# Transposing a block's gradient row into two PSUM banks, and issuing two zero fills earlier

## The chip, the cores and the metric

The kernel runs on one NeuronCore of a Trainium2 chip. The metric is the device time of one execution in microseconds. A core has a matrix engine (PE), a vector engine (DVE), a scalar engine (ACT), a general engine (POOL) and a queue engine (SP). Each takes its instructions in order. Transfers between device memory and the on-chip memory (SBUF) are carried by 16 DMA engines, which serve a queue that POOL fills and a queue that SP fills. Results of PE land in PSUM, which has eight banks of 2 KB per partition.

## The reference

One decode step of a conditioned transformer block with a single token, forward and backward. The token's vector has 1024 elements. A vector `c` gives six modulation vectors; attention of 32 heads over the last 4096 of 65536 cached positions (4 key and value heads) follows, then a gated feed-forward part with 3584 hidden units.

```python
def _B_ref(x, w_gate, w_up, w_down):
    g = jnp.einsum('bsd,df->bsf', x, w_gate)
    u = jnp.einsum('bsd,df->bsf', x, w_up)
    h = _sigmoid(g) * u
    return jnp.einsum('bsf,fd->bsd', h, w_down)
mod = (_silu(c) @ w_mod).reshape(c.shape[0], 6, 1, -1)
...
h = _layernorm(x, axis=-1) * (1 + ca) + sa
x = x + ga * _A_ref(h, A_k_cache, A_v_cache, A_wq, A_wo)
h = _layernorm(x, axis=-1) * (1 + cb) + sb
x = x + gb * _B_ref(h, B_w_gate, B_w_up, B_w_down)
...
_out, _vjp = jax.vjp(_f, A_x, A_k_cache, A_v_cache, A_wq, A_wo, B_w_gate, B_w_up, B_w_down, c, w_mod)
_grads = _vjp(grad_out)
```

The outputs are the block's output and the gradients of ten inputs. The gradients of the two caches have the shape of the whole caches, 2 x 4 x 65536 x 128 elements in bf16, and are zero outside the last 4096 positions. Writing these zeros is most of the kernel's traffic.

## The kernel before

The code is written out by hand in program order, and each engine runs its share in that order. One large SBUF array, `arena`, holds all big tiles at fixed offsets, so a tile that is to be written again waits for the transfer that reads it.

**Zero fills.** `zero(n, after)` takes the next `n` regions from one list, `zleft`, and issues each as a POOL transfer (L209) of 1 MB from an SBUF tile of zeros to device memory. At six places of the list stands a narrow region: a counter reset, a transfer of 2.5 KB (L194) and one of 960 KB (L197). With `after` given, the fill waits for that instruction. The tables at the top (`Z_FFN`, `Z_ROWS`, `Z_HAND` and others) say how many fills are issued at each place. A fill earlier in the program therefore means one fewer at the place where the list ends.

**Feed-forward turns.** The hidden units are cut into seven blocks of 512. For each block `q`, `load_ug` (L965, POOL) brings its columns of w_up and w_gate in four transfers of 512 KB, into one of two buffers, and `load_wd` (L954, SP) brings its rows of w_down in two. `front(q)` (L1053, PE) multiplies the gate and up columns with the vector `h2`. `turn(q)` then makes the gates, transposes three of the eight row groups of the loaded weights (`turned`, L1076), sums w_down times the output gradient on DVE (`wd_ttr`, L253, into the tile `dhh`), and calls `dug_part(q)`.

**The gradient row.** `dug_part` computes eight columns `dug` (four for up, four for gate), turns each into a row that stands on all 128 partitions by a PE transpose of a broadcast column (L1111), and copies the result from PSUM to the SBUF tile `dug_b` (which is the tile `scr` in the profile). ACT copies the first 512 elements (L1113) and DVE the second 512 (L245). In the turns, PSUM tiles for such work come from two banks in turn (`new_tp`, with `rot` holding `psum` and `prq`). The transposes of other tiles that fill idle PE time are called side units (`side`, L939 on PE, L940 on ACT).

After the turn, DVE multiplies five of the row groups of the block's weights with `dug_b` and sums them (L253 into `dh2acc`). That frees the block's buffer, and the loads of block `q + 2` are issued. The loop issues fills between them:

```python
            if j == 3:
                if q + 2 < NB:
                    load_ug(q + 2, 0, 4, (0,))
                    zero(Z_FFN[q][0])
                    load_ug(q + 2, 0, 4, (1,))
...
        if q + 2 < NB:
            load_ug(q + 2, 4, 4, (0,))
            zero(Z_FFN[q][1])
            load_ug(q + 2, 4, 4, (1,))
            turn(q + 1, Z_FFN[q][2])
```

In `turn`, the fills of its argument are issued as `zero(fills, wd_ttr(2, 3))`, behind the last w_down sum.

**End stage.** After the seventh block the kernel writes the weight gradients: outer products on DVE (L249) followed by POOL stores, `dwd` (L1138), `dw_rows` (L1130), `dwo` (L1265), then the modulation gradients `sec` (L1260), the gradients of the caches (L1308 for values, L1304 for keys) and of wq. `zero(Z_ROWS[i])` stands behind the i-th of several `dw_rows` calls: `Z_ROWS[0]` behind the second one (about 449 us in the profile) and `Z_ROWS[1]` behind the third (about 459 us).

Of the kernel before, what the change touches and what calls it, by code (L numbers as in the profile page):

```python
# [10 lines left out]
P = 128  # L11
# [11 lines left out]
FB = 512  # L23
# [30 lines left out]
Z_N = spread(33, 128)  # L54
Z_B = [n + (i in (31, 38)) for i, n in enumerate(spread(29, 43))] + [1, 1, 1, 1, 0] + [1, 0, 0, 1, 1, 1, 0, 0] + [1, 0, 1, 0, 1, 0, 0, 0]
Z_FOLD = (1, 1, 2, 3)
Z_FFN = [(1, 0, 1)] + [(1, 1, 1)] * 4 + [(0, 2)]
Z_HAND = (1, 2, 1, 1, 1)
Z_ROWS = (1, 1, 0, 0, 0, 0, 0, 0)
JT = 3  # L60
JV = KD - JT
@with_exitstack
def kernel(
# [26 lines left out]
    nc = tc.nc  # L90
# [17 lines left out]
    def vt(shape, name, dt=FP32):  # L108
        return pool.tile(shape, dt, name=name)
# [13 lines left out]
    ident_bf = vt([P, P], "ident_bf", BF16)  # L123
# [61 lines left out]
    def zero(n, after=None, big=False):  # L185
        for _ in range(n):
            if len(zleft) <= keep[0]:
                return
            region, narrow_ = zleft.pop(0)
            first = None  # L190
            if narrow_:
                nc.gpsimd.inc_swdge_sem([], [], mode="reset_dge_cursor")
                n = nlen - ncount.pop()
                first = nc.gpsimd.dma_start(  # L194
                    out=rest[0:NS, 0:nlen * 128].rearrange("p (t x) -> p t x", t=2)[:, :, n * 64:(n + 1) * 64],
                    in_=zeros[0:NS, 0:64].rearrange("p (t x) -> p t x", t=1).broadcast_to([NS, 2, 64]))
                ins = nc.gpsimd.dma_start(  # L197
                    out=region[8:P, :].bitcast(FP32).rearrange("(t p) x -> p t x", t=2),
                    in_=zeros[0:60, :].rearrange("p (t x) -> p t x", t=1).broadcast_to([60, 2, ZW // 2]))
            elif 119 - len(zleft) in UNEVEN:  # L200
                first = ins = uneven(region)
            elif big and region.shape[0] == 1:
                ins = nc.gpsimd.dma_start(  # L203
                    out=as_rows(region, BIGP).bitcast(FP32),
                    in_=zero_src[:, 0:P * ZW // 4].rearrange("i (p x) -> (i p) x", p=BIGP).bitcast(FP8))
            else:
                if region.shape[0] == 1:
                    region = as_rows(region, P)
                ins = nc.gpsimd.dma_start(out=region.bitcast(FP32), in_=zeros[:, :])  # L209
            if after is not None:  # L210
                dep(first or ins, after)
# [5 lines left out]
    def next_pool():  # L217
        nrot[0] += 1
        return rot[nrot[0] % len(rot)]
# [11 lines left out]
    def new_tp(name="tp"):  # L231
        p, tag = next_pool()
        return p.tile([P, 1024], BF16, name=name, tag=tag)
# [4 lines left out]
    def mulv(out, a, b):  # L238
        return tt(out, a, b, ALU.mult)
# [4 lines left out]
    def cp(out, a):  # L244
        return nc.vector.tensor_copy(out=out, in_=a)  # L245
# [94 lines left out]
    def bcast(col_bf, ncols, out_bf, engs):  # L340
        for k, j0 in enumerate(range(0, ncols, 4)):
            ps = new_ps("bc_ps")
            for jj in range(4):
                nc.tensor.matmul(ps[:, jj * P:(jj + 1) * P],
                                 lhsT=col_bf[:, j0 + jj:j0 + jj + 1].broadcast_to([P, P]), rhs=ident_bf[:, :],
                                 start=(jj == 0), stop=(jj == 3), skip_group_check=True)
            o = out_bf[:, j0 * P:(j0 + 4) * P]
            if engs[k % len(engs)] == "A":
                last = nc.scalar.copy(out=o, in_=ps[:, :])
            else:  # L350
                last = cp(o, ps[:, :])
        return last
# [229 lines left out]
    for tb in range(4):  # L582
# [3 lines left out]
        tp = new_tp("tp_pT")  # L586
# [7 lines left out]
    last = nc.vector.reciprocal(out=rsum, in_=ssum)  # L594
# [318 lines left out]
    v = A3_ps[:, 0:48].rearrange("p (j n) -> p j n", j=KD)  # L913
# [48 lines left out]
    def load_ug(q, j0, n, ks=(0, 1)):  # L962
        for k in ks:
            view = (wu_view, wg_view)[k]
            nc.gpsimd.dma_start(out=ug_tile(q, k, j0, n), in_=ug_part(view, q, j0, n))  # L965
# [72 lines left out]
    dug_b = scr  # L1038
# [66 lines left out]
    def dug_part(q):  # L1105
        dug = dug_all[:, 8 * q:8 * q + 8]
        mulv(dug[:, 0:4], small["dhh"], small["sg"])
        mulv(dug[:, 4:8], small["dhh"], small["hom"])
        tp = new_tp("tp_dug")
        for i in range(8):  # L1110
            nc.tensor.transpose(tp[:, i * P:(i + 1) * P], dug[:, i:i + 1].broadcast_to([P, P]), ident_bf[:, :])  # L1111
        o, v = dug_b.rearrange("p (k f i) -> p k f i", k=2, i=4), tp.rearrange("p (k i f) -> p k f i", k=2, i=4)
        nc.scalar.copy(out=o[:, 0, :, :], in_=v[:, 0, :, :])  # L1113
        return cp(o[:, 1, :, :], v[:, 1, :, :])

    dug_row = [ar(o, 7) for o in (24, 152)]
    def dug_rows(k):
# [9 lines left out]
    def dw_rows(k, j, off, outer):  # L1127
        t = ar(off, 7)
        outer(t, h2[:, j:j + 1], dug_row[k])
        nc.gpsimd.dma_start(out=(dwu_view, dwg_view)[k][:, j, :], in_=t)  # L1130

    def dwd(q, off, outer):
        t = ar(off, 8).rearrange("p (i d) -> p i d", i=4)
        for i in range(4):
            outer(t[:, i, :], hh_all[:, 4 * q + i:4 * q + i + 1], b1k)

        def store():
            nc.gpsimd.dma_start(out=wd_dram(out_8, q), in_=t)  # L1138
        return store
# [7 lines left out]
    def turn(q, fills=0):  # L1147
        gates()
        turned(q, range(JT - 1))
        wd_ttr(0)  # L1150
        hh_ops(q)
        first = wd_ttr(1)
        ffn_mm(q, 0)
        if q + 1 < NB:
            load_wd(q + 1, 0, 2)
        ffn_mm(q, 2)
        turned(q, (JT - 1,))
        side(1)
        zero(fills, wd_ttr(2, 3))
        if q + 1 < NB:  # L1160
            load_wd(q + 1, 2, 2)
        last = dug_part(q)
        turned_mm(q)
        side(1)
        return first, last
# [6 lines left out]
    for q in range(NB):  # L1172
# [8 lines left out]
        for j in range(JT, KD):  # L1181
            w = ug_flat(q, j)
            ttr(w, w, dug_b, dh2acc[:, q * JV + j - JT:q * JV + j - JT + 1])
# [5 lines that stand above are left out]
                elif more:  # L1189
                    zero(Z_FFN[q][1])  # L1190
                    dwd(0, 24, outer_dve)()
# [4 lines left out]
# [5 lines that stand above are left out]
        elif more:  # L1201
# [23 lines left out]
    dw_rows(0, 1, 16, outer_dve)  # L1225
    zero(Z_ROWS[0])
    bcast(dattn_bf, KD, dattn_b, "V")
# [34 lines left out]
    def dwo(u):  # L1262
        for a in range(4):
            outer_dve(wo_t[u][:, a, :], o_perm[:, 8 * a + u:8 * a + u + 1], dattn_b)
        nc.gpsimd.dma_start(out=wo_dram(out_5, u), in_=wo_t[u])  # L1265
# [50 lines left out]
    for b in range(2):  # L1316
        do4 = new_ps("do4")
        for i in range(KD):
            for a in range(4):
# [4 lines left out]
                       in_=do4.rearrange("q (a h r) -> q a h r", a=4, h=4))  # L1324
# [6 lines left out]
    dw_rows(0, 2, 40, outer_dve)  # L1331
    zero(Z_ROWS[1])
    dwo(2)
# [14 lines left out]
    dw_rows(0, 4, 32, outer_dve)  # L1348
    zero(Z_ROWS[2])
    dwo(3)  # L1350
    dw_rows(0, 5, 176, outer_dve)
    dw_rows(0, 6, 160, outer_dve)
    zero(Z_ROWS[3])
    dw_rows(0, 7, 40, outer_dve)
# [10 lines left out]
    dw_rows(1, 0, 64, outer_dve)  # L1365
    zero(Z_ROWS[4])
    dw_rows(1, 1, 72, outer_dve)
# [9 lines left out]
    dw_rows(1, 2, 80, outer_dve)  # L1377
    zero(Z_ROWS[5])
    dw_rows(1, 3, 16, outer_dve)
# [136 lines left out]
```

## Time and profile before

| What | Value |
|---|---|
| median of three runs | 594.79 us (594.39 to 596.32) |
| the profiled execution: its own time | 594.57 us |
| its span, first to last instruction | 592.8 us |
| PE, DVE, ACT, POOL busy | 430.4, 354.9, 248.1, 145.9 us |
| transfers | 246.58 MB, mean 416 GB/s |
| read from and written to device memory | 79.17 MB and 185.60 MB |
| 1 MB zero fills L209 | 42, median 12.6 us from issue to landing |
| transposes of `dug` (L1111) | 56, first at 329.6 us, last at 430.8 us |

The profile is one execution; its times are counted from the start of the span. Transfers are counted per queue and per issuing line, and the time from issue to landing includes the wait behind transfers that were issued before. A line number can be that of a helper: L245 is every DVE copy, L249 every scaled outer product, L253 every multiply-and-sum.

### The profile page before, as it was taken

Reading aid. Unit: us, or ns where it says so; the run is one execution under the profiler, and the core shown is the slowest. Engines: PE = TensorE matmul, PEld = TensorE weight load, DVE = VectorE, ACT = ScalarE, POOL = GpSimd, SP = SyncE. Lnnn points to the kernel's source line nnn. Section 1 sums busy time; section 2 is a strip of 40 time slices with the busy share of each in tenths; the row PEclk is TensorE's granted clock in tenths of the full one; section 3 lists DMA queues with packets and bytes.
Section 4 is the critical chain, followed back from the end, with each engine's and each line's share of the span. In section 5 each row is a group of like instructions: output and inputs, shape, how many; then the busy total and the mean of one; then the engine's idle time right before and its main releaser. Section 6 shows DMA issues by size and latency. Waiting matters only on the chain.

```text
span 592.8 us, 10216 instructions
## 1 busy us (share of the span) xinstructions
PE 430.4 (73%) x4196; PEld 245.4 (41%) x4196; DVE 354.9 (60%) x647; ACT 248.1 (42%) x398; POOL 145.9 (25%) x251
## 2 busy tenths in 40 slices
PE   3997789999999999997977757776655446084510
PEld 2784433333334545543544545555442445013100
DVE  3665679988930102039373866887986869536750
ACT  2579511554540103411224635665671455093410
POOL 3112213122122212122222331323222433213100
PEclk9998689999999999998998757777785658555555
DMA  8999999999999999999999999999999999999997
GB/s 348 421 420 421 422 465 426 425 422 429 426 404 461 417 438 421 410 420 435 427 395 409 418 412 407 397 408 410 423 422 426 424 425 425 422 408 418 414 417 302
DMA packets 32048, 246.58 MB, mean 416 GB/s; under 512 B 4782, under 2 KB 4782, under 8 KB 16689
## 3 DMA queue, kind: packets, MB, share of 16 engines
q0 software_dynamic: 27008, 226.51, 94.8%
q1 hardware_dynamic: 4944, 19.41, 9.2%
q8 instruction: 33, 0.54, 0.4%
q14 instruction: 15, 0.11, 0.0%
q10 hardware_dynamic: 48, 0.01, 0.0%
HBM read 79.17 MB, written 185.60 MB: 447 GB/s over the span
## 4 chain that ended last, share of the span: by engine, by line
PE 35%; DMA 33%; DVE 16%; ACT 6%; issue 6%; POOL 1%; ACTq 0%; POOLq 0%; DVEq 0%
DMA out_dram<-arena 12%; PE b_ps L796 11%; PE n_ps L737 9%; DMA arena<-in_w_mod_dram 6%; DMA arena<-in_B_w_gate_dram 5%; DVE arena L249 4%; PE t_ps L685 4%; DMA out_dram<-out_dram 3%; DVE arena L253 3%; DMA arena<-in_B_w_up_dram 3%; ACT arena L524 2%; DVE scr L253 2%; DVE arena L236 2%; DMA arena<-in_B_w_down_dram 2%; PE tp_k L503 1%
## 5 line engine op out<-in xcount | busy, mean ns | idle before, releaser
L796 PE MATMUL b_ps<-arena 128*128 128x512 bf16 x512 | 118.6, 384 | 1.1 <-ACT arena L940 1.1
L940 ACT COPY arena<-tp_side 128x1024 bf16<-128x1024 bf16 x62 | 60.9, 1017 | 53.0 <-PE tp_side L939 52.2
L236 DVE TENSOR_TENSOR arena<-arena 128x2048 bf16<-128x2048 bf16 x64 | 77.7, 1224 | 8.8 <-PE n_ps L737 5.1
L796 PEld LDWEIGHTS <-arena 128*128 128x128 bf16 x512 | 49.0, 99 | 58.0 <-issue 5.4
L737 PE MATMUL n_ps<-arena 128*128 128x512 bf16 x256 | 67.7, 389 | 3.4 <-DVE arena L236 2.9
L203 POOL DMA_DIRECT2D out_dram<-out_dram x72 | 35.7, 496 | 127.4 <-PE n_ps L737 57.3
L939 PE MATMUL tp_side<-ident_bf,arena 128*128 128x128 bf16 x496 | 50.6, 270 | 9.6 <-DVE arena L236 5.3
L939 PEld LDWEIGHTS <-arena 128*128 128x128 bf16 x496 | 42.0, 124 | 18.4 <-issue 9.1
L1295 PE MATMUL ps_kv<-arena 32*128 32x512 bf16 x64 | 26.6, 581 | 27.6 <-DVE arena L257 11.7
L693 ACT CAST arena<-t_ps 128x512 bf16<-128x512 f32 x56 | 28.9, 598 | 39.9 <-PE t_ps L685 39.9
L1299 ACT ACTIVATE arena<-ps_kv 128x512 bf16<-128x512 f32 x48 | 25.0, 714 | 39.6 <-PE ps_kv L1295 20.5
L253 DVE CUSTOM_DVE_ANT_0 arena<-arena,scr 128x1024 bf16<-128x1024 bf16 x35 | 40.8, 1218 | 0.2
L737 PEld LDWEIGHTS <-arena 128*128 128x128 bf16 x256 | 21.4, 99 | 35.6 <-issue 19.4
L209 POOL DMA_DIRECT2D out_dram<-zeros x42 | 23.2, 554 | 52.4 <-DVE rows_all L236 22.9
L253 DVE CUSTOM_DVE_ANT_0 scr<-arena,b1k 128x1024 bf16<-128x1024 bf16 x28 | 34.2, 1222 | 2.8 <-DMA arena<-in_B_w_down_dram 2.4
L245 DVE CAST arena<-b_ps 128x512 bf16<-128x512 f32 x6 | 4.1, 692 | 50.2 <-PE b_ps L796 50.2
L249 DVE TENSOR_SCALAR arena<-arena,h 128x3584 bf16<-128x3584 bf16 (+1 forms) x24 | 28.3, 1191 | 7.9 <-DMA out_dram<-arena 7.8
L685 PE MATMUL t_ps<-arena 128*32 128x512 bf16 x256 | 24.1, 399 | 2.8 <-ACT arena L760 2.8
L1295 PEld LDWEIGHTS <-arena 32*128 32x128 bf16 x64 | 6.8, 112 | 46.2 <-issue 45.4
L249 DVE TENSOR_SCALAR arena<-arena,cs_col 128x4096 bf16<-128x4096 bf16 (+1 forms) x16 | 16.0, 1015 | 15.2 <-DMA out_dram<-arena 15.2
L524 ACT COPY arena<-tp_wq 128x1024 bf16<-128x1024 bf16 x23 | 21.4, 1066 | 7.3 <-PE tp_wq L522 7.3
L1077 ACT COPY arena<-tp_ug 128x1024 bf16<-128x1024 bf16 x21 | 20.5, 1008 | 6.7 <-PE tp_ug L1076 6.7
(326 smaller groups left out, 660.3 us busy)
## 6 DMA issues: line engine op xcount, KB each, us to landing
out_dram<-zeros POOLq DMA_DIRECT2D x42, 1024.0 KB, 12.6
out_dram<-arena POOLq DMA_DIRECT2D x35, 1024.0 KB, 15.0
out_dram<-arena POOLq DMA_DIRECT2D x16, 896.0 KB, 17.3
arena<-in_A_wq_dram POOLq DMA_DIRECT2D x8, 1024.0 KB, 21.0
arena<-in_A_wo_dram POOLq DMA_DIRECT2D x8, 1024.0 KB, 13.3
arena<-in_w_mod_dram POOLq DMA_DIRECT2D x7, 1024.0 KB, 19.0
arena<-in_B_w_up_dram POOLq DMA_DIRECT2D x14, 512.0 KB, 11.5
arena<-in_B_w_gate_dram POOLq DMA_DIRECT2D x14, 512.0 KB, 14.5
```

Source lines behind the costliest of these rows:

```text
L203: ins = nc.gpsimd.dma_start(out=as_rows(region, BIGP).bitcast(FP32), in_=zero_src[:, 0:P * ZW // 4].rearrange("i (p x) -> (i p) x", p=BIGP ...
L236: return nc.vector.tensor_tensor(out=out, in0=a, in1=b, op=op)
L249: return nc.vector.tensor_scalar(out=out, in0=a, scalar1=s1, scalar2=None, op0=op0)
L253: return nc.vector.tensor_tensor_reduce(out=out, in0=w, in1=b, scale=1.0, scalar=0.0, op0=ALU.mult, op1=ALU.add, accum_out=acc)
L524: nc.scalar.copy(out=blk, in_=tp[:, :])
L685: nc.tensor.matmul(ps[32 * hh:32 * hh + 32, :].rearrange("p (j m) -> p j m", j=4), lhsT=N_sb[:, h * P + a:(h + 1) * P - 3 + a:4], rhs=a4[: ...
L693: nc.scalar.copy(out=o, in_=v)
L737: mm = nc.tensor.matmul(nbank[k][:, :], lhsT=k_nat[:, g, t_ * DH:(t_ + 1) * DH], rhs=vp[:, t_ % 2, 4 * k:4 * k + 4, :].rearrange("p h d -> ...
L796: mm = nc.tensor.matmul(bbank[p][k][:, :], lhsT=a4[:, p, h, :], rhs=wo_t[u][:, a, k * 512:(k + 1) * 512], start=(i == 0 and a == 0), stop= ...
L939: nc.tensor.transpose(tp[:, i * P:(i + 1) * P], blk[:, i * P:(i + 1) * P], ident_bf[:, :])
L940: nc.scalar.copy(out=blk if dst is None else dst, in_=tp[:, :])
L1295: nc.tensor.matmul(ps[:, :], lhsT=rows[r, t8 * P:(t8 + 1) * P], rhs=bd[r, :], start=True, stop=True, tile_position=(32 * tc_, 0))
```

## The change

`dug_part` takes two PSUM tiles in place of one. Four transposes go into the first, and ACT copies it; four go into the second, and DVE copies it. Instructions, shapes and destinations stay the same; the source rows are now in different banks.

Two entries of the fill tables change. Turn 1 and turn 2 issue two fills instead of one behind their w_down sums, and the two fills behind the second and third `dw_rows` are no longer issued. The total stays the same. As all fills come from one list in order, the regions written in between shift by one or two places, two of the narrow ones among them.

```diff
-Z_FFN = [(1, 0, 1)] + [(1, 1, 1)] * 4 + [(0, 2)]
+Z_FFN = [(1, 0, 2), (1, 1, 2)] + [(1, 1, 1)] * 3 + [(0, 2)]
 Z_HAND = (1, 2, 1, 1, 1)
-Z_ROWS = (1, 1, 0, 0, 0, 0, 0, 0)
+Z_ROWS = (0, 0, 0, 0, 0, 0, 0, 0)
...
         mulv(dug[:, 4:8], small["dhh"], small["hom"])
-        tp = new_tp("tp_dug")
-        for i in range(8):
-            nc.tensor.transpose(tp[:, i * P:(i + 1) * P], dug[:, i:i + 1].broadcast_to([P, P]), ident_bf[:, :])
-        o, v = dug_b.rearrange("p (k f i) -> p k f i", k=2, i=4), tp.rearrange("p (k i f) -> p k f i", k=2, i=4)
-        nc.scalar.copy(out=o[:, 0, :, :], in_=v[:, 0, :, :])
-        return cp(o[:, 1, :, :], v[:, 1, :, :])
+        o = dug_b.rearrange("p (k f i) -> p k f i", k=2, i=4)
+        for k in range(2):
+            tp = new_tp("tp_dug")[:, 0:FB]
+            for i in range(4):
+                nc.tensor.transpose(tp[:, i * P:(i + 1) * P], dug[:, 4 * k + i:4 * k + i + 1].broadcast_to([P, P]),
+                                    ident_bf[:, :])
+            v = tp.rearrange("p (i f) -> p f i", i=4)
+            last = nc.scalar.copy(out=o[:, k, :, :], in_=v) if k == 0 else cp(o[:, k, :, :], v)
+        return last
```

The new code is three lines longer, so a line behind it has a number that is 3 higher in the changed kernel (L1265 becomes L1268).

## The prediction

> **What bounds the kernel now.** I read the transfers first, because the table of slices has every engine idle for part of the time and the transfers never.
>
> ```profile
> DMA  8999999999999999999999999999999999999997
> GB/s 348 421 420 421 422 465 426 425 422 429 426 404 461 417 438 421 410 420 435 427 395 409 418 412 407 397 408 410 423 422 426 424 425 425 422 408 418 414 417 302
> ```
>
> Each digit is the busy share of the 16 DMA engines in one fortieth of the span (14.8 us). Only the first and the last slice are under nine tenths. So the span is about bytes over rate: 246.58 MB at the mean of 416 GB/s is 592.7 us of the 592.8. An edit that leaves the bytes alone can only change the rate, or a gap in the stream.
>
> Next the stretches around the change: PE, PEld, DVE, ACT and POOL busy, then granted clock, DMA share and GB/s.
>
> ```profile
> 340.00:360.00 20.00, 11.95 (x164) 9.68 (x164) 11.42 (x26) 8.64 (x10) 6.16 (x9) 0.57 1.15 415
> 360.00:380.00 20.00, 13.10 (x224) 10.68 (x222) 17.79 (x37) 14.20 (x20) 4.64 (x7) 0.80 1.11 397
> 380.00:400.00 20.00, 15.11 (x220) 12.61 (x221) 15.35 (x34) 11.79 (x16) 5.97 (x9) 0.67 1.13 407
> 440.00:460.00 20.00, 10.50 (x107) 5.40 (x107) 15.21 (x47) 5.34 (x5) 5.57 (x9) 0.66 1.07 425
> ```
>
> The feed-forward turns (about 320 to 444) move 397 to 415 GB/s, the start of the end stage 425. Then the chain of waits in the turns, start and length in us:
>
> ```profile
> 357.23 15.78 DMA arena<-in_B_w_gate_dram
> 373.00 0.04 issue
> 373.04 1.10 PE fg L1053 x16
> ...
> 380.56 1.05 PE tp_dug L1111 x8
> 381.61 0.03 ACTq L1113
> 381.63 0.04 issue
> 381.67 0.59 ACT scr L1113
> 382.27 0.02 issue
> 382.29 0.70 DVE scr L245
> ...
> 390.42 14.39 DMA arena<-in_B_w_gate_dram
> ```
>
> A turn starts when its gate weights land, runs to the free buffer, and asks for the weights of two blocks later. Half of this loop is a transfer of 512 KB that takes 14 to 16 us, although 512 KB at 425 GB/s is 1.2 us: it stands in line behind what was issued before it. Its landing is set by the line, not by the moment of its issue. Last, how long the line is (issue to landing, shortest, median, longest):
>
> ```profile
> DMA to landing us min/median/max: 7.1/10.2/15.8
> DMA to landing us min/median/max: 10.7/12.0/14.6
> DMA to landing us min/median/max: 17.0/17.3/17.9
> ```
>
> These are the weight loads L965 from 349 to 412, the zero fills L209 from 440 to 462, and the row stores L1130 from 478 to 512. The line never empties. It is shortest, 7.1 us, for the load issued at 370.19, and full from about 470: there POOL issues one store per 2.44 us, mostly released by an earlier store's landing.
>
> **The change, part by part.**
>
> *Two banks.* Per turn PE makes the same eight transposes (1.05 us together), ACT the same copy (586 ns), DVE the same copy (692 ns). Before, the DVE copy starts when the ACT copy ends (382.29 against 381.67); the built program of the changed kernel makes it wait for PE instead. It can start at about 381.67, and ACT's some 0.5 us earlier. That takes 382.29 - 381.67 = 0.62 us out of each of 7 turns, 4.3 us of chain. Two copies at once from two banks run undisturbed where the trace has them: 597 ns on ACT and 683 on DVE for the ps_kv banks. The second tile takes the other of the two rotating banks, whose last user is the side unit's copy (378.79 to 379.81), done before the transposes at 380.56: no new wait there. If that copy were late, PE and the 24 small matmuls of `turned_mm` behind it would wait up to one such copy, 1.0 us a turn; DVE would still be ahead or even. What is late next? The weights. The freed buffer lets POOL issue L965 0.62 us earlier into a line 7 to 16 us long, so it lands when its place comes up. In turns 1 to 4 I count nothing. From 404.85 on the chain is DVE's to 443, so turns 5 and 6 do bring 2 x 0.62 = 1.2 us of earlier stores; these join a line of 8.3 us at its shortest there (the store of 434.39), so the end gets nothing.
>
> *Two fills moved.* A 1 MB fill takes the line 2.44 us. The second one in turn 1 goes in behind that of 346.68, the second one in turn 2 behind that of 365.89; POOL spends 0.56 us on each, and both stand before loads that POOL cannot issue for 3.7 us more (its idle time <-DVE dh2acc). All fills come from one list, so the 960 KB fill with its small extra transfer moves from 380.6 to 370.9, ahead of a gate load: 0.7 us more of POOL, hidden by the line. The loads behind land 2.44 us later after turn 1 and 4.9 later after turn 2, and the gates wait for them, so the turns end 4.9 - 1.2 = 3.7 us later. SP's w_down loads have their own queue, wait for the same sums, and shift along.
>
> Then the end stage has 4.9 us less to move: POOL no longer issues the fills of 449.62 and 459.20. All bytes ahead of the store of 460.18 are the same in both kernels, so from there on the stream stands at the same absolute time, if it was never empty. Is it? At 449 to 460 the line is 10.7 to 14.6 us; less 4.9 it is at least 5.8. DVE is 100% busy from 460 to 470 and then waits for landings (2.05, 1.30 and 0.26 us up to 478.70), which is where its lateness is absorbed; what is left meets the 17 us line. So the two 4.9 us cancel. The bounds of this term are -0 and +3.7 (nothing given back); I take 0, since its nearest row is the line of 5.8 us that stays.
>
> *The thin place.* From 366 to 376 the stream moves 386 GB/s, against 411 in the nine us before and 406 in the fourteen after (408 weighted): (408 - 386) x 10 / 408 = 0.54 us lost. The extra fills stand just there. Between 0 and 0.54 us I take 0.5.
>
> The end is that of the slowest of the 16 engines: after the POOL queue's last landing at 587.1 the SP queue's last store lands at 591.9, and in the end stage the 16 completions of a store are spread over 4.2 us. If only the leaders ran thin at 366 to 376, the 0.5 us is not theirs to give, and the term is 0. The Trainium skill ("DMA: Bandwidth & Descriptors", Latency and other measured facts) says that engines 7 and 15 are usually slower than the others in traces. By that rule the sum would be 594.6 instead of 594.1; the spread agrees with unequal engines, and no row here names them.
>
> **Sum.** The profiled execution took 594.57 us, its span 592.8 and 1.77 around it; the median of the three runs is 594.79. 594.57 - 0.5 (thin place) + 0 (fills) + 0 (copies) = 594.1. A measurement of this kernel tells about 0.3%, 1.8 us, from no change.
>
> **Rivals.**
>
> *Faster: the turns are thin throughout.* From 320 to 420 the stream moves 407 GB/s on average against 425 after: 100 x 18 / 425 = 4.2 us lost. If that comes from short lines and not from the weight loads themselves, the extra megabytes and earlier issues win back much of it: half is 592.5, all is 590.4. For it: the turns' line of 7.1 us, and nowhere else a rate so low for so long. Against it: 340 to 360 has loads that wait 15 us and still only 415.
>
> *Slower: the end stage does not give the time back.* The turns end 3.7 us later, and the stores of 449 to 460 come one by one from DVE, which waits there for buffers (1.43 and 2.93 us <-DMA out_dram). With 5.8 us of line left and a 4.2 us spread, the leading engines have 1.6 us in hand. This decides once the stores come more than 1.6 us later than the stream: the leaders then run dry, and with the slow ones tied to the same late stores the delay stays. Price up to 3.7: 598.3; half is 596.4. For it: the fills stood there as padding between buffer-bound stores. Against it: the 17 us line afterwards. The Trainium skill ("DMA: Bandwidth & Descriptors", Anatomy of one DMA) prices a transfer at about 2.0 us plus bytes over 436 GB/s, an estimate of 4.4 us for 1 MB. By it the turns would end 8.8 - 1.2 = 7.6 us late, and this rival would reach 602.2. The trace does not agree inside a full line: the stores from 478 on pass at 2.44 us each.
>
> *The change does nothing:* DVE still waits for ACT through the shared tile `scr`. Then 4.3 us of chain stay, and by the fills alone it is 594.1 to 594.6, still no difference. The built program speaks against it.
>
> **Numbers.** Forecast (no measurable difference, own range 593.0 to 595.6) 0.41, the change that does nothing 0.05, faster rival 0.31, slower rival 0.23. So faster 0.31, same 0.46, slower 0.23. Cases of both signs hold over half, so the range reaches half-way and a little more into each: 591.2 (past 592.5) to 597.2 (past 596.4). About a tenth stays out on each side.
>
> **What would show it.** DVE's copy of tp_dug released by PE and not by ACT, 1.10 us idle before it in place of 1.72: the first step. Gates of blocks 4 and later waiting for loads some 4.9 us later: the second. Over 386 GB/s at 366 to 376: the third. The store after the dropped fills (L1268, before 460.18) landing within 1 us of 473.7, and the line at 450 to 462 between 5 and 10 us: the cancelling. A stream under nine tenths there, or a line near 4 us, makes the slower rival; over 415 GB/s through all turns the faster one.

## The result: slower by a seventh of a per cent

| Kernel | Median | Runs | Lowest to highest |
|---|---|---|---|
| before | 594.61 us | 22 | 593.09 to 596.32 |
| changed | 595.45 us | 22 | 594.63 to 596.34 |

The ratio is 1.0016, with a 95% interval of [1.0008, 1.0023]: a small loss, 0.84 us by the medians, but a real one. The forecast was no measurable difference at 594.1 us. The profiled execution of the changed kernel took 594.71 us (span 592.9), which is near the low end of its own runs, so its trace shows less than the whole loss; e2_fills and e7_hand below have profiles near their medians and show the rest. In the table below, one run each of e2, e5, e7, e9 and e15 and two of e12 took 598.8 to 601.7 us and make those intervals wide, so that the medians stand for the typical run.

First the table of slices of the changed kernel, the share of the 16 DMA engines and the GB/s in fortieths of the span.

```profile
DMA  8999999999999999999999999999999999999998
GB/s 350 419 420 420 425 471 417 424 421 421 434 403 462 421 433 426 407 418 435 422 407 404 419 409 413 415 410 404 410 423 425 415 416 411 414 400 425 416 412 336
```

The share is still nine tenths or more in all slices but the first and the last. But slices 32 to 36 (460 to 534 us) move 415, 416, 411, 414 and 400 GB/s, where before had 424, 425, 425, 422 and 408. The stretches of the changed kernel, with the columns of before's table:

```profile
340.00:360.00 20.00, 12.41 (x183) 9.84 (x180) 13.11 (x28) 10.44 (x14) 6.06 (x10) 0.74 1.15 413
360.00:380.00 20.00, 11.96 (x200) 9.62 (x198) 14.93 (x33) 11.66 (x18) 5.98 (x9) 0.76 1.15 414
440.00:460.00 20.00, 11.57 (x108) 7.63 (x110) 16.22 (x47) 8.71 (x10) 4.69 (x8) 0.59 1.09 426
...
463.00:487.00 24.00, 11.05 (x174) 9.98 (x175) 21.77 (x47) 13.96 (x16) 11.06 (x15) 0.64 1.00 412
487.00:500.00 13.00, 11.26 (x205) 10.27 (x207) 10.01 (x16) 9.30 (x16) 3.90 (x7) 0.62 1.01 411
500.00:523.00 23.00, 6.48 (x44) 1.83 (x37) 13.64 (x22) 5.61 (x13) 5.46 (x10) 0.65 1.01 415
523.00:532.00 9.00, 9.00 (x20) 1.87 (x19) 3.81 (x5) 9.00 (x21) 1.55 (x2) 0.50 1.02 393
```

and the last four of these for the kernel before:

```profile
463.00:487.00 24.00, 9.51 (x154) 8.70 (x152) 18.61 (x35) 11.54 (x16) 9.71 (x12) 0.57 1.03 426
487.00:500.00 13.00, 11.14 (x217) 9.20 (x215) 10.20 (x16) 9.63 (x16) 3.69 (x7) 0.82 1.01 421
500.00:523.00 23.00, 4.88 (x13) 1.09 (x12) 11.93 (x20) 4.01 (x9) 6.37 (x10) 0.61 1.01 423
523.00:532.00 9.00, 9.00 (x19) 1.78 (x18) 3.39 (x3) 9.00 (x20) 1.55 (x2) 0.50 1.01 398
```

The turns gained (360 to 380: 414 for 397 GB/s), the end stage lost (463 to 523: 411 to 415 for 421 to 426), and the share of DMA time in these stretches is 1.00 to 1.01 in the changed kernel (a share over 1 means that packets overlap in time). Over a whole stretch nothing ran dry. A short place did, which the long stretches hide; here are its four microseconds, changed and then before:

```profile
463.00:467.00 4.00, 1.89 (x28) 1.77 (x29) 4.00 (x12) 3.08 (x3) 1.65 (x3) 0.90 0.97 404
463.00:467.00 4.00, 3.26 (x55) 3.02 (x53) 4.00 (x11) 2.66 (x4) 2.41 (x3) 0.50 1.06 422
```

This is part of what 463 to 487 lost, where the share is 1.00 for 1.03. In the stretches from 487 to 523 it is 1.01 again. The transfers' own view says the same for 500 to 523, before and then changed:

```profile
DMA packets 1453, 9.72 MB, mean 423 GB/s; under 512 B 161, under 2 KB 161, under 8 KB 1012
q0 software_dynamic: 1451, 9.70, 101.1%
```

```profile
DMA packets 1427, 9.54 MB, mean 415 GB/s; under 512 B 154, under 2 KB 154, under 8 KB 1029
q0 software_dynamic: 1426, 9.52, 101.0%
```

The same share of the engines' time carries fewer bytes: each packet takes longer. The trace has the time of every packet, and 16 completions for every transfer, as many as there are engines. It doesn't name the engines: "the leading engines" and "the last engine" below are read from the first and the last of these completions. A row store is cut into packets of 8 KB or 7 KB; undisturbed they take 309 and 272 ns. Averaged by bytes and per 8 KB, those of 480 to 500 us take 313 ns before and 320 ns after. At 523 to 530 there is also a burst of packets of some 606 ns, twice the usual time: 19 before, 33 after. Summed over the packets of 8 KB and 7 KB from 456 us on and divided by 16, the time above 309 or 272 ns is 2.30 us before and 3.08 us after. That is 0.78 us more for the mean engine. It is not yet the loss in time: the end is set by the last engine, and these two executions differ by only 0.14 us, since in the execution of before the last engine loses 1.7 us in its burst.

### The profile page after: what moved, and what is told of

It is laid out like the page before. It is cut to its first block, busy times and chain, and to the rows that moved or that the text cites. A ratio compares the mean times of both kernels' runs of the same rounds, so it can differ in the third digit from the quotient of the medians.

```text
span 592.9 us, 10217 instructions
## 1 busy us (share of the span) xinstructions
PE 435.8 (74%) x4196; PEld 248.5 (42%) x4196; DVE 354.7 (60%) x647; ACT 247.8 (42%) x398; POOL 144.2 (24%) x251
## 4 chain that ended last, share of the span: by engine, by line
PE 39%; DMA 27%; DVE 17%; ACT 7%; issue 5%; POOL 1%; ACTq 0%; POOLq 0%; DVEq 0%
PE b_ps L796 14%; DMA out_dram<-arena 13%; DMA arena<-in_B_w_gate_dram 9%; PE n_ps L737 9%; DVE arena L236 4%; DVE arena L249 4%; PE t_ps L685 4%; DMA out_dram<-out_dram 3%; DVE arena L253 3%; ACT arena L524 2%; DVE scr L253 2%; DMA out_dram<-zeros 2%; PE tp_side L939 1%; PE tp_k L503 1%; PE do L1324 1%
## 5 line engine op out<-in xcount | busy, mean ns | idle before, releaser
L796 PEld LDWEIGHTS <-arena 128*128 128x128 bf16 x512 | 49.0, 99 | 58.0 <-issue 5.4
L939 PE MATMUL tp_side<-ident_bf,arena 128*128 128x128 bf16 x496 | 52.0, 278 | 10.7 <-DVE arena L236 5.8
L939 PEld LDWEIGHTS <-arena 128*128 128x128 bf16 x496 | 43.9, 128 | 19.0 <-issue 9.8
L1298 PE MATMUL ps_kv<-arena 32*128 32x512 bf16 x64 | 26.6, 581 | 26.2 <-DVE arena L257 10.2
L737 PEld LDWEIGHTS <-arena 128*128 128x128 bf16 x256 | 21.4, 99 | 35.7 <-issue 19.4
L1053 PE MATMUL fg<-arena,h_bf 128*32 128x256 bf16 x224 | 15.0, 404 | 11.2 <-DMA arena<-in_B_w_gate_dram 11.2
```

Source lines behind the costliest of these rows:

```text
L737: mm = nc.tensor.matmul(nbank[k][:, :], lhsT=k_nat[:, g, t_ * DH:(t_ + 1) * DH], rhs=vp[:, t_ % 2, 4 * k:4 * k + 4, :].rearrange("p h d -> ...
L796: mm = nc.tensor.matmul(bbank[p][k][:, :], lhsT=a4[:, p, h, :], rhs=wo_t[u][:, a, k * 512:(k + 1) * 512], start=(i == 0 and a == 0), stop= ...
L939: nc.tensor.transpose(tp[:, i * P:(i + 1) * P], blk[:, i * P:(i + 1) * P], ident_bf[:, :])
L1298: nc.tensor.matmul(ps[:, :], lhsT=rows[r, t8 * P:(t8 + 1) * P], rhs=bd[r, :], start=True, stop=True, tile_position=(32 * tc_, 0))
```

## The experiments

Before is measured again in each group of runs; each ratio is against the runs of its own group. "Late fills" are the landings of zero fills after 460 us; the ns are the mean per 8 KB of the store packets that start in those stretches; "burst" counts 8 KB packets over 550 ns at 520 to 534 us.

| Kernel | Median, before (us) | Ratio, 95% interval | Late fills land at | ns 480-500 | ns 500-520 | Burst |
|---|---|---|---|---|---|---|
| before | | | 464, 471 | 313 | 312 | 19 |
| changed | 595.45, 594.61 | 1.0016 [1.0008, 1.0023] | none | 320 | 318 | 33 |
| e1_banks | 593.91, 594.20 | 0.9990 [0.9979, 1.0002] | 464, 471 | 313 | 312 | 19 |
| e2_fills | 595.86, 594.20 | 1.0027 [1.0006, 1.0047] | none | 318 | 320 | 31 |
| e3_fold | 594.53, 594.20 | 1.0004 [0.9991, 1.0017] | 464, 471 | 315 | 315 | 22 |
| e4_four | 596.95, 594.20 | 1.0042 [1.0028, 1.0056] | none | 324 | 322 | 39 |
| e5_later | 593.01, 594.59 | 0.9986 [0.9967, 1.0005] | 488, 497 | 324 | 310 | 0 |
| e6_reorder | 595.62, 594.59 | 1.0021 [1.0009, 1.0032] | none | 319 | 318 | 29 |
| e7_hand | 595.57, 594.59 | 1.0025 [1.0007, 1.0044] | none | 319 | 320 | 32 |
| e8_best | 593.78, 594.59 | 0.9990 [0.9978, 1.0002] | 464, 476 | 313 | 311 | 19 |
| e9_late | 593.48, 594.39 | 0.9997 [0.9980, 1.0015] | 488, 497 | 324 | 310 | 0 |
| e10_copy | 593.84, 594.39 | 0.9995 [0.9984, 1.0005] | 488, 497 (copies) | 321 | 310 | 0 |
| e11_one | 593.82, 594.39 | 0.9992 [0.9983, 1.0001] | 497 | 322 | 311 | 12 |
| e12_split | 593.23, 594.39 | 0.9997 [0.9976, 1.0018] | 488, 515 | 319 | 316 | 0 |
| e13_small | 595.29, 594.59 | 1.0017 [1.0006, 1.0027] | 497 (one eighth) | 320 | 318 | 34 |
| e14_keep | 595.38, 594.59 | 1.0013 [1.0004, 1.0023] | 461, 468, 489, 517 | 318 | 315 | 0 |
| e15_onebank | 593.10, 594.59 | 0.9988 [0.9967, 1.0008] | 488, 497 | 323 | 311 | 1 |
| e16_third | 593.70, 594.59 | 0.9984 [0.9975, 0.9993] | 462, 469, 515 | 313 | 316 | 0 |
| e17_fold2 | 592.77, 594.49 | 0.9974 [0.9963, 0.9985] | 466, 495, 515 | 318 | 316 | 0 |
| e18_fold1 | 592.79, 594.49 | 0.9972 [0.9963, 0.9981] | 462, 469, 508 | 313 | 316 | 0 |

### One half of the change at a time

e1_banks has the two PSUM banks and the fills of before; e2_fills has the fills of the change and the single PSUM tile of before.

```diff
 # e1_banks, against the changed kernel
-Z_FFN = [(1, 0, 2), (1, 1, 2)] + [(1, 1, 1)] * 3 + [(0, 2)]
+Z_FFN = [(1, 0, 1)] + [(1, 1, 1)] * 4 + [(0, 2)]
-Z_ROWS = (0, 0, 0, 0, 0, 0, 0, 0)
+Z_ROWS = (1, 1, 0, 0, 0, 0, 0, 0)
```

> The two banks alone, all fills where they were. The end-stage theory (the fills taken from 449 and 459 us are what costs) and the turns theory (the fills put into the turns are what costs) both expect no loss: 0 to 0.5 us faster than before, and DVE's copy of the row released by PE. The banks theory (the new order of banks makes PE, ACT or DVE later somewhere) expects the whole loss of the change here: 0.8 us slower than before.

> The two fills alone, one bank. The end-stage theory and the turns theory expect the whole loss of the change: 0.8 us slower than before, or more (to 1.4), with the leading DMA engines short of work near 464 us and a stream of about 413 GB/s from 460 to 520 under the first, and about 401 GB/s at 400 to 420 under the second. The banks theory expects no difference from before.

The banks alone stay within 0.1% of before; the fills alone are 1.66 us slower. The loss is the fills'.

### Is it the later turns, or the missing fills of the end stage?

e3_fold puts the same extra fills into turns 1 and 2 but takes them from the fold at about 325 us, so that the end stage keeps both of its own. e4_four moves two more fills from the start of the end stage into turns 3 and 4.

```diff
 # e3_fold, against the changed kernel
-Z_FOLD = (1, 1, 2, 3)
+Z_FOLD = (1, 1, 2, 1)
-Z_ROWS = (0, 0, 0, 0, 0, 0, 0, 0)
+Z_ROWS = (1, 1, 0, 0, 0, 0, 0, 0)
 # e4_four, against the changed kernel: two more out of 442 to 449, into turns 3 and 4
-Z_FFN = [(1, 0, 2), (1, 1, 2)] + [(1, 1, 1)] * 3 + [(0, 2)]
-Z_HAND = (1, 2, 1, 1, 1)
+Z_FFN = [(1, 0, 2), (1, 1, 2), (1, 1, 2), (1, 1, 2), (1, 1, 1), (0, 2)]
+Z_HAND = (1, 2, 1, 0, 0)
```

> The change, but the two extra fills of turns 1 and 2 are taken from the three issued in turn 0 instead of from the end stage, whose two fills stay. The end-stage theory expects the thin place at 366 to 376 filled as in the change and no loss at 460 to 520: 0.5 to 1.0 us faster than before. The turns theory expects the loss to stay, 0.8 us slower than before, since turns 1 and 2 issue what they issue in the change. The banks theory expects 0.8 us slower too.

> The change with two more fills moved, those of 438 and 444 us, into turns 3 and 4. The end-stage theory expects the leading engines to run dry earlier and longer, from about 445: 2 to 3 us slower than before. The turns theory expects twice the loss of the change, 1.6 us slower. The banks theory expects the loss of the change, 0.8 us. If full lines in the turns are a gain and nothing is lost in the end stage, it is faster than the change.

e3 shows no loss, though its turns have the extra fills. Its interval, [0.9991, 1.0017], doesn't shut one out; its packets do better, with 310 ns at 470 to 480 where the changed kernel's take 318. e4, with two fewer fills at the end, is the slowest of all (596.95), and from 500 to 520 its packets are the slowest too (322 ns). It also runs dry in earnest, as the theory of the end stage expected:

```profile
460.00:464.00 4.00, 2.57 (x36) 1.05 (x32) 3.93 (x14) 1.30 (x1) 1.16 (x2) 0.77 0.80 334
```

Yet the store issued at 465.30 there, the first of the output projection's gradient, has its first completion 2.4 us later than in before and its last 0.1 us earlier: what ran dry were the leading engines. The last engine falls behind only with the packets that follow, by 2.0 us up to 524. What counts is what the end stage has lost, not what the turns have gained; e7_hand below, with the turns of before, settles it.

### Where in the end stage

e5_later puts the two fills behind the fifth and seventh row store of the first gradient in place of the second and third. e6_reorder keeps the change and moves two stores of the output projection's gradient ahead of the row store that waits for buffer 40. e7_hand leaves the turns as before and issues the two fills at 444, ahead of that row store. e8_best is e1 with the reordering of e6.

```diff
 # e5_later, against e1_banks
-Z_ROWS = (1, 1, 0, 0, 0, 0, 0, 0)
+Z_ROWS = (0, 0, 1, 1, 0, 0, 0, 0)
 # e7_hand, against e1_banks
-Z_HAND = (1, 2, 1, 1, 1)
-Z_ROWS = (1, 1, 0, 0, 0, 0, 0, 0)
+Z_HAND = (1, 2, 1, 1, 3)
+Z_ROWS = (0, 0, 0, 0, 0, 0, 0, 0)
 # e6_reorder against the changed kernel, e8_best against e1_banks
+    dwo(2)
+    dwo(0)
     dw_rows(0, 2, 40, outer_dve)
     zero(Z_ROWS[1])
-    dwo(2)
-    dwo(0)
```

> Two banks, turns as before; the two fills of 449 and 459 us are issued later in the end stage, behind the fourth and sixth of the further row stores (about 472 and 478). The end-stage theory: the line of transfers is 4.9 us shorter at 460 although nothing went into the turns, the leading engines run short there, and the packets of 470 to 520 take about 318 ns instead of 312: 0.7 to 1.2 us slower than the two banks alone, so 0.4 to 0.9 slower than before. The turns theory: nothing is changed in the turns, so as fast as the two banks alone, 0.3 us faster than before.

> The change, with the outer products and stores dwo(2) and dwo(0) put ahead of dw_rows(0, 2, 40), where DVE stood 2.9 us idle for the buffer at offset 40. The end-stage theory: these two megabytes pad the line at 458 to 462 as the fills had done, packets of 470 to 520 take about 312 ns again, and the loss is gone: as fast as the two banks alone, 0.3 us faster than before (0 to 0.8). The turns theory: the loss stays, 0.8 us slower than before.

> Two banks, turns as before; the two fills of 449 and 459 us are issued only a little earlier, at 444, but now ahead of the store whose landing frees the buffer at offset 40. The end-stage theory: that landing comes 4.9 us later, DVE's stores from 460 on with it, and nothing stands in the line behind it: the loss of the change, 0.8 to 1.2 us slower than the two banks alone, 0.5 to 0.9 slower than before. The turns theory: as fast as the two banks alone, 0.3 us faster than before.

> Two banks, all fills as before, and dwo(2) and dwo(0) ahead of dw_rows(0, 2, 40). The end-stage theory: the line was long enough at 460 before, so more of it brings nothing: equal to the two banks alone, 593.9 (593.5 to 594.3). If the line's length at 460 still cost something there, it is faster than that by up to 0.5 us.

These overturned the theory of that moment, that a short line at 460 us is what costs the time. The line is equally short in e5 (the first of a store's 16 completions comes 3.8 us after the issue at 458 to 463, the last 7.7 us) as in the changed kernel and in e7, and e5 is fast. In e7 DVE waits for a buffer longest of all, one line of its timeline (start, duration, and in brackets the idle time before it and its releaser):

```profile
461.78 1.15 DVE L249 TENSOR_SCALAR arena<-arena,h 128x3584 bf16<-128x3584 bf16 x1 [7.83 <-DMA out_dram<-arena]
```

and the DMA share is 0.96 from 463 to 467, but 1.00 to 1.02 in the three stretches from 463 to 523. e5 has such a place too (0.96 and 405 GB/s at 456 to 460), so a short time without work for some engines isn't the loss by itself. e7 is 0.98 us slower than before with the turns of before, so the loss doesn't need the extra fills in the turns either. e6 makes the line longer (4.5 and 9.7 us) and stays at 318 to 319 ns, and slow. e8, with that order and the fills of before, is as fast as e1. What sets e5 apart from these is in its stretches:

```profile
463.00:487.00 24.00, 11.05 (x199) 10.03 (x196) 19.56 (x39) 12.12 (x17) 11.09 (x14) 0.64 1.03 416
487.00:500.00 13.00, 9.64 (x141) 7.20 (x142) 9.24 (x13) 8.60 (x13) 4.16 (x6) 0.87 1.04 421
500.00:523.00 23.00, 4.06 (x8) 0.79 (x8) 11.54 (x20) 3.55 (x8) 5.78 (x10) 0.52 1.01 427
523.00:532.00 9.00, 9.00 (x20) 1.78 (x18) 5.37 (x6) 9.00 (x20) 1.62 (x3) 0.50 1.02 425
```

e5 starts at the changed kernel's rate (416 GB/s for 412). Its two fills land at 487.6 and 496.8. While they pass, packets are slower still (335 ns at 492 to 496); from 500 on they take 310 ns, the stream moves 427 GB/s, and the burst of 523 to 530 isn't there (425 GB/s for 393). So the new theory: once the stores have become slow they stay slow, until a zero fill passes through the queue among them. (In the changed kernel they are back at 309 to 311 ns from 530 to 546, behind two loads of 256 KB.)

### Does a passing fill end the slow packets?

e9_late is the changed kernel with two fills more held back for 487 and 497 us. e10_copy is e5 with these two as copies from DRAM to DRAM. e11_one holds back one fill instead of two. e12_split is e5 with the second fill 18 us later. e15_onebank is the kernel before, one PSUM tile, with the fills of e5.

```diff
 # e9_late, against the changed kernel
-Z_FOLD = (1, 1, 2, 3)
-Z_ROWS = (0, 0, 0, 0, 0, 0, 0, 0)
+Z_FOLD = (1, 1, 2, 1)
+Z_ROWS = (0, 0, 1, 1, 0, 0, 0, 0)
 # e10_copy, against e5_later (and the same for Z_ROWS[3])
-    zero(Z_ROWS[2])
+    zero(Z_ROWS[2], None, True)
 # e11_one, against the changed kernel
-Z_FOLD = (1, 1, 2, 3)
-Z_ROWS = (0, 0, 0, 0, 0, 0, 0, 0)
+Z_FOLD = (1, 1, 2, 2)
+Z_ROWS = (0, 0, 0, 1, 0, 0, 0, 0)
 # e12_split, against e1_banks
-Z_ROWS = (1, 1, 0, 0, 0, 0, 0, 0)
+Z_ROWS = (0, 0, 1, 0, 0, 0, 1, 0)
 # e15_onebank, against the kernel before
-Z_ROWS = (1, 1, 0, 0, 0, 0, 0, 0)
+Z_ROWS = (0, 0, 1, 1, 0, 0, 0, 0)
```

> The changed kernel with two more fills held back from the two-block end of the gradient sums and put among the row stores at about 487 and 497 us (the fills in turns 1 and 2 stay as the change has them). If store packets run slow until some other transfer passes, the two late fills end the slow stretch: packets of about 310 ns from about 490 on in place of 318 to 324, and 593.0 to 593.8 us, faster than the kernel before or level with it. If what costs the time is the later end of the turns, or anything before 480 us, the late fills change nothing: 595.2 to 595.8.

> Two banks, the turns' fills as before, and the two fills at 487 and 497 us as copies from DRAM to DRAM in place of writes from a zeroed tile. If any transfer that isn't a row store ends the slow packets, this runs like the version with writes: about 593.0 us. If it takes one that reads little (the write's source is one small tile), the packets stay at 318 to 324 ns and the copies' own reads cost some 2 us more: 595 or later.

> The changed kernel with one late fill instead of two (at about 497 us). If a single passing fill ends the slow packets, they are about 310 ns from 500 on: some 0.7 of the 1.2 us that the change loses comes back after that, 594.0 to 594.8. If it takes two, or fills have nothing to do with it: 595.2 to 595.8.

> Two banks, the turns' fills as before, one late fill at about 487 us and the second some 20 us later instead of 10. If each fill ends the slow packets for some tens of us, the stretch from 490 to 540 stays at about 310 ns throughout and the time is at or a little below that of the version with fills at 487 and 497: 592.5 to 593.2. If only the fact of two fills matters, 593.0 as there; if fills have nothing to do with it, 593.9 as with two banks alone, or 595.

> One bank as before, the turns as before, and the two fills of 449 and 459 moved to 487 and 497. If late fills act by themselves, without the two banks, this is faster than the kernel before by what the two-bank version with the same fills gains over the banks alone, 0.5 to 1.0 us: 593.4 to 594.2. If the gain came from the banks and the fills together, it is at 594.5 or later.

In all five the packets do as the theory has it; four of the times missed their ranges, e11 and e15 by up to 0.3 us to the fast side, e12 by 0.03 us and e10 by 0.8 us to the slow side. e9 keeps the change's turns, and its median is 0.91 us below its before, where the changed kernel's is 0.84 above: two fills that pass late undo the loss. One does nearly as much (e11, 0.57 below), and e11's interval, [0.9983, 1.0001], lies wholly under the changed kernel's. That they gain more than the loss is seen in the medians alone. The kind of transfer doesn't matter for the packets (e10: 310 ns after 500), though with copies, which also read, the kernel is 0.55 us below its before, and with fills in the same places (e5) 1.58 below. In e12 the fill that lands at 488 is enough to bring the packets to 310 to 317 ns until the second passes (325 to 341 ns at 510 to 514); behind that one they stay at 309 to 315 up to 560, and there is no burst. In e15 the late fills act without the two banks, and as much as with them (593.10 against 593.01).

### How little has to pass, and is the turns' line a limit?

e13_small is the changed kernel with 16 of the 128 rows of one fill kept back from turn 2, one packet for each engine, and issued at 481. e14_keep and e16_third keep the early fills of the end stage and take late ones from the last turns.

```diff
 # e13_small, against the changed kernel; later[0] is the kept part of turn 2's second fill
-    zero(Z_ROWS[3])
+    nc.gpsimd.dma_start(out=later[0].bitcast(FP32), in_=zeros[112:P, :])
 # e14_keep, against e1_banks
-Z_FFN = [(1, 0, 1)] + [(1, 1, 1)] * 4 + [(0, 2)]
-Z_ROWS = (1, 1, 0, 0, 0, 0, 0, 0)
+Z_FFN = [(1, 0, 1)] + [(1, 1, 1)] * 2 + [(1, 1, 0)] * 2 + [(0, 2)]
+Z_ROWS = (1, 1, 1, 0, 0, 0, 1, 0)
 # e16_third, against e1_banks
-Z_FFN = [(1, 0, 1)] + [(1, 1, 1)] * 4 + [(0, 2)]
-Z_ROWS = (1, 1, 0, 0, 0, 0, 0, 0)
+Z_FFN = [(1, 0, 1)] + [(1, 1, 1)] * 3 + [(1, 1, 0)] + [(0, 2)]
+Z_ROWS = (1, 1, 0, 0, 0, 0, 1, 0)
```

> The changed kernel with one eighth of one fill (16 of its 128 rows, one packet for each transfer engine) kept back from turn 2 and put among the row stores at about 497 us. If any break in the row of equal stores ends the slow packets, this does it like a whole fill: packets of 310 to 312 ns after 500, no burst of 606 ns packets at 523 to 530, 593.8 to 594.5 us. If it takes a fill's 2.4 us, the packets stay at 318 and the time at 595.2 to 595.8.

> Two banks, the two early fills of the end stage where the kernel before has them (444 to 460), and two fills taken from the last turns and put at 487 and 515. If the slow packets begin with the short line at 460 and late fills end what is left, this has neither: packets near 310 from 470 to 540, 592.0 to 593.2 us. If the turns miss the fills that are taken out of them, or late fills are only a cure for a line that was short, it is at the two banks alone: 593.7 to 594.3.

> Two banks, the two early fills of the end stage kept, and one fill taken from the last turn and put at about 515. The kernel with two banks alone has its packets at 310 to 313 up to 520, then a burst of 606 ns packets at 523 to 530; if a fill that passes shortly before takes the burst away, this saves some 0.4 us of it and more in the packets after: 593.2 to 593.7 us. If the burst comes anyway: 593.8 to 594.2.

One packet for each engine isn't enough: e13 stays at 318 ns, with a burst of 34. e14 was a miss, for a reason of its own. Its end stage is as fast as hoped (425 GB/s at 500 to 532), but the stretch at the end of the turns is this:

```profile
430.00:442.00 12.00, 8.91 (x116) 7.78 (x113) 11.18 (x24) 9.88 (x12) 3.22 (x5) 0.79 0.94 361
```

Without its fills the last turn lets the queue run empty: 361 GB/s, a DMA share of 0.94 and not above 1, and a store issued at 433.39 that lands 4.5 us later (its first completion comes after 4.1). The last engine is 1.3 us late from there on. This is what running dry looks like when it reaches all engines; in the changed kernel's end stage it reaches the leading ones alone. e16, which takes one fill from there, loses 0.4 us at that place in the mean of the engines and is at the upper edge of what was expected.

The Trainium skill ("DMA: Bandwidth & Descriptors", Anatomy of one DMA) prices a transfer at about 2.0 us plus bytes over 436 GB/s, an estimate of 4.4 us for 1 MB. In e14's empty queue the trace agrees, with 4.5 us; in a full one the stores pass every 2.44 us.

### A version that beats both

e17_fold2 and e18_fold1 have the two banks, the turns and early fills of before, and take two late fills, or one, from the fold at about 325 us.

```diff
 # e17_fold2, against e1_banks
-Z_FOLD = (1, 1, 2, 3)
-Z_ROWS = (1, 1, 0, 0, 0, 0, 0, 0)
+Z_FOLD = (1, 1, 2, 1)
+Z_ROWS = (1, 1, 0, 1, 0, 0, 1, 0)
 # e18_fold1, against e1_banks
-Z_FOLD = (1, 1, 2, 3)
-Z_ROWS = (1, 1, 0, 0, 0, 0, 0, 0)
+Z_FOLD = (1, 1, 2, 2)
+Z_ROWS = (1, 1, 0, 0, 0, 1, 0, 0)
```

> Two banks, the turns and the early fills of the end stage as before, and two of the three fills of the fold (about 325 us) put at 497 and 515 instead. If the short line at 460 begins the slow packets and late fills end what is left, packets are near 310 from 470 to 540 with no burst of 606 ns packets, and nothing is lost in the turns: 592.3 to 593.2 us. If the fills are missed where they are taken out, or the end stage has no more to give than two late fills gave it: 593.0 to 594.0.

> The same with one late fill only, at about 507 us, shortly before the burst at 523 to 530. If one fill that passes there takes the burst away: 592.8 to 593.6 us. If it takes two: 593.6 to 594.2, as with the two banks alone.

Both came out as expected under the theory: 592.77 us (ratio 0.9974 [0.9963, 0.9985]) and 592.79 us (0.9972 [0.9963, 0.9981]), 1.7 us below before in the same group, where the changed kernel was 0.84 above. Two stretches of e17:

```profile
500.00:523.00 23.00, 3.68 (x8) 0.77 (x8) 9.41 (x17) 3.17 (x7) 6.21 (x10) 0.50 1.03 427
523.00:532.00 9.00, 9.00 (x20) 1.82 (x19) 5.08 (x6) 9.00 (x20) 1.55 (x2) 0.50 1.01 425
```

The runs are also closer together: 592.45 to 593.11, where before in the same group has 593.04 to 595.87. The burst may be part of that width; two profiles point to it. Between the landings at 524 and 530 the last engine of before's profiled execution (594.57 us) loses 1.7 us to it; in e1's profiled execution (593.11 us) the burst is as large by count but falls on engines that are ahead, and the last one loses nothing.

## Why the prediction was wrong, step by step

**Two banks: right.** The chain of waits no longer has DVE behind ACT, and DVE's copy is released by PE, as the tile's view of the changed kernel shows (copies, then who ended the idle time of their engines, in us and times):

```profile
L245 DVE COPY scr<-tp_dug x7: 691/691/692, 332.4 to 435.7; 128x512 bf16<-128x512 bf16 x7
...
  PE tp_dug L1113: 15.3, 13
```

DVE sits idle 1.05 to 1.06 us before it in six turns and 1.25 us in one; 1.10 was forecast. The step was to be worth nothing at the end, and no run tells it from nothing: e1 is at 0.9990 [0.9979, 1.0002], and e15 and e5, the same fills with one bank and with two, are 0.1 us apart.

**Fills in the turns: right.** The turns end later. The chain's gate weights of 392.82 land 17.08 us after issue, at 409.90; before, those of 390.42 landed at 404.81. That is 5.1 us, against 4.9 forecast. The line is longer in the turns and as long as before at 478 to 512; from issue to landing, these are the loads L965 from 349 to 412 of the changed kernel, and then the row stores:

```profile
DMA to landing us min/median/max: 9.3/13.0/17.4
DMA to landing us min/median/max: 16.6/17.6/17.8
```

**The cancelling: it came at 474, and the sum failed behind it.** The store that comes after the dropped fills (issued at 460.18 before, 465.00 now) lands at 473.61 us, before at 473.68. So the two 4.9 us did cancel there, for the engine that lands last. The step that failed is the next sentence, "from there on the stream stands at the same absolute time, if it was never empty".

Its condition held for the last engine and not for the leading ones. The prediction took the whole waiting line, 5.8 us, as work in hand, and gave the leaders 1.6 us of it. But a 1 MB store that enters an empty queue takes 4.1 us to its first completion and 4.5 us to its last (e14), so little of the 5.8 us was work. Also, 10.7 to 14.6 was the row of the fills; the store of 458.60 landed after 10.2 us, with its first completion after 5.94. The same store, issued at 463.41 now, has its first completion after 3.76 us, which is as from an empty queue (an estimate from e14's 4.1 us, less eight packets of 272 in place of 309 ns, is 3.8). Its last comes after 7.7. The sign named for the cancelling, a line of 5 to 10 us at 450 to 462, was met by the store of 459.36 alone (9.6); those of 450.62 and 453.91 still took 13.8 and 12.6. The leaders came out of it 0.4 us later than in before, and the last engine on time.

What the last engine lost, it lost later, with a queue that was full again: its packets had become slower, and from 487 to 523 us the stream moved 411 to 415 GB/s in place of 421 to 423. The sum had no term for that. The leading engines lose first. The 16 completions of a store, 3.7 us apart for the store of 465.00, are 2.8 apart by 499; before they stay 4.2 to 4.3 apart. The last engine, which sets the end, is on time until about 499 us; it then loses 0.4 us by 510 in the profiled execution, and in e2, whose profile is near its median, 1.1 us by 524 and 0.4 more in the burst. The term "two fills moved" was taken as 0; measured, it is +1.66 us without the banks (e2), and with them some 1.1, the change's +0.84 less the -0.29 of e1, which is itself within the noise. Its bounds, 0 to +3.7, held both. I took the end of the range whose row, the waiting line, tells whether the engines have work, and not how long a packet takes.

**The thin place: filled, but worth nothing at the end.** From 366 to 376 the stream moves 411 GB/s for 386, and in the mean of the engines it is ahead by 1.0 us at 396. It gives 0.7 of this back by 425 (400 to 420: 401 GB/s for 413). At 430 to 435 the last completions of the same transfers come 4.9 us later than before, the time of the two added fills (2 x 2.44), and none of the gain; the first ones come 2.8 to 3.2 us later. The prediction named that case, leaders only and a term of 0, and preferred 0.5; it was 0.

**The rivals.** The slower one had the right place and sign, and the medians of the changed kernel and e2 lie between nothing and half of its price, and the first half of its mechanism came true: the leaders ran dry. The second half, that the slow engines are tied to the same late stores and the delay stays, did not: in the changed kernel and even in e4 the last engine lands on time at 474, and e5, which is as short of work at 460, is fast. e14 has the whole mechanism, in another place. The faster rival fails at 400 to 420, where the turns move 401 GB/s with the longer line. The change did what it says.

**What stays open.** That a fill which passes at 485 us or later ends the slow packets is shown, with and without the change, with one bank and two. What starts them isn't. In twelve kernels a store issued at 458 to 464 had its first completion within 3.7 to 4.5 us, and all of these had 317 to 321 ns at 470 to 480; in the other eight, with 5.2 us or more, packets were at 309 to 311 ns at 476 to 480. The place where leading engines run dry goes with it: worked out from the packets' times, the DMA share of some two microseconds between 449 and 470 falls to 0.85 to 0.99 (0.62 in e4) in each of the twelve, and under 1 in none of the eight. But these eight are also the ones with fills that pass at 460 to 476, so the short line, the dry place and the missing fill weren't told apart. Nor does any fill do: one landed at 459.8 in the changed kernel, and its packets were slow at 470. That the engines hinder one another when they come nearer in step is an idea that fits the shrinking spread; no run settles it. Nor is it settled why the burst comes only after slow or unbroken stores.

## What to carry to other kernels

A time from issue to landing is not all waiting: take off what a transfer needs in an empty queue, and read the first completion too, since it tells of the leading engines. And a busy queue is not a queue at full speed: before a term is set to zero because the line stays full, look at bytes for each busy microsecond of the engines, stretch by stretch and in short stretches too, and at packet times. Count the term as unknown where the change alters what stands next to what. Filler traffic that can go anywhere is worth placing inside long runs of equal stores, as long as the place it is taken from keeps its line; here a single 1 MB fill moved to the right place brought the changed kernel some 1.4 us (e11, each against its own before), and two of them taken out of the last turns cost more than they brought (e14).

## What was not expected of the hardware

- The same 8 KB store packet takes 309 ns or, for tens of microseconds at a time, 316 to 324 ns on average, with a DMA share of 1.01; the stream moves 411 to 415 GB/s in place of 421 to 427.
- A 1 MB fill or a DRAM-to-DRAM copy that passes at 485 us or later brought the packets back to 310 to 317 ns for 20 us and more (e12, e5); while it passes they take up to 341 ns, in means of 2 us (e5, e12). A transfer of one packet for each engine did not (e13), nor did the fill that landed at 459.8 in the changed kernel keep them fast.
- Where 256 KB loads follow the stores in the same queue (at about 525 us), 19 to 39 of the last store packets took over 550 ns, most of them 606, unless a fill had passed in the 30 us before; then 0 or 1, and 12 in e11.
- The lead of some engines over the others is no lasting property: the spread of a store's 16 completions shrank from 4.7 to 2.4 us in the changed kernel and grew from 4.5 to 6.0 us in the burst of before, and here a gain, or a time without work, that only the leaders had was not seen in the last engine.
